# Two pairs with unscaled queries, a last pair normalized bank by bank, and conversions that begin one quarter sooner

## The chip, the cores and the metric

The kernel runs on one core of one Trainium2 chip. The metric is the time of the core on the device in microseconds, the median of three runs. Times of the trace are counted from the start of the profiled span.

## The reference, cut to what matters

Three stages follow each other: causal attention over 2 x 12 heads of 448 tokens, a soft mixture of 8 experts over the 896 tokens, and a gated feed-forward stage. What the change touches is the first one:

```python
scores = scale * np.matmul(q, k.transpose(0, 1, 3, 2))      # scale = 1/sqrt(64) = 0.125
scores = np.where(mask, -1000000000.0, scores)
scores = scores - np.max(scores, axis=-1, keepdims=True)
attn = np.exp(scores)
attn = attn / (np.sum(attn, axis=-1, keepdims=True) + 1e-09)
return np.matmul(attn, v)
```

The inputs are float32. The weights of the feed-forward stage (`wab`, `wo`) reach the kernel as 64-bit words.

## The kernel before, in words

**Pairs and quarters.** Attention works on 12 pairs of heads, one head in partitions 0 to 63 and one in 64 to 127. A pair's score matrix has seven blocks of 64 query rows, i = 0 to 6, of 64(i+1) columns each, packed into four PSUM banks, `BANKS = ((6, 0), (5, 1), (4, 2), (3,))`. The loop over `it` (0 to 12) and `g` (0 to 3) is written out in a fixed order (manual schedule): what stands first in the program runs first on its engine. One turn (it, g), below a quarter, computes bank g of pair `it` and turns a quarter of pair it-1:

- `scores`: a bf16 matmul puts the mask into the bank, TensorE (PE) adds q times k, and VectorE (DVE) takes the negated maximum of each block into `nm` (line 261).
- `softmax`: ScalarE (ACT) writes exp(score + nm) into `p` and the row sums into `sm` (line 273).
- `norm`: DVE makes the reciprocals `rc` (lines 285, 286), GpSimd (POOL) multiplies the blocks of `p` by them (line 289). At g = 2 blocks of banks 0 and 1 are normalized together, at g = 3 those of bank 2, and bank 3 in the next pair's quarter 0.
- `transp`: PE transposes four 128x128 blocks of the pair before into a PSUM tile `t`, in the order `TORD = (1, 3, 0, 2)`. `t_1` needs blocks 4, 5, 6, 2 of `p`; `t_3` blocks 4, 5, 6; `t_0` and `t_2` also need block 3, which is bank 3. ACT evicts three of the four to `pT` (line 307), DVE evicts `t_3` at the end of quarter 1 (line 311).
- `pv`, `xtr`, `logits`: PE multiplies `pT` with v two pairs behind (in four steps kt; the second reads `t_2`, the last two read `t_3`), transposes the result and adds to the logits of the experts.

**Queries.** `begin(it)` multiplies q by 0.125 in place (line 236): DVE does it for pair 0, POOL for the others, one pair ahead.

**Conversions.** The 64-bit weight words are widened to fp32 in between. One conversion of a raw tile is two ACT passes of 128x768 (lines 163, 164) and, one conversion later (`LAG = 1`), two DVE passes (lines 194, 197). `conv_step` is called in every quarter after the first `CVOFF`, and three of four quarters hold one conversion (`CVN`): the first of 32 in quarter (1, 3), the last in (12, 0). A conversion behind (11, 3) uses POOL instead of ACT (lines 156, 159). A raw tile that DVE is done with frees a slot, and `pump` issues the next load on the SP queue, in a fixed order: raw tiles 0 to 31, then the experts' weights `w`.

**The start.** SP issues q and k of pair 0, v, a raw tile, a `w`, q and k of pair 1, and more. PE first runs 32 `warm` matmuls on a bf16 copy of the identity (`ident16`, made by DVE on line 105), then the scores of pair 0, and four `warm` matmuls ahead of each quarter of pair 1.

**Behind attention.** `pv(11)`, `xtr(11)`, the last logits and the softmax over tokens follow each other down to `ssum` (line 587), the experts' input, and then the experts run on `w` tiles as they arrive. Two of the slots for `w`, t0 and t1, open where the tiles that `ssum` reads are closed, so that the SP queue, which is in order, waits for `ssum` there.

Of the kernel before, what the change touches and what calls it, by code (L numbers as in the profile page):

```python
# [15 lines left out]
ALU = mybir.AluOpType  # L16
# [3 lines left out]
S = 448  # L20
# [3 lines left out]
BANKS = ((6, 0), (5, 1), (4, 2), (3,))  # L24
# [13 lines left out]
TDVE = 1  # L38
# [4 lines left out]
    (("rect", 28, 4, 0, 28), ("tri", 6, 2), ("sq", 28, 4)),  # L43
    (("sq", 8, 16),),
)
CVOFF = 7
NWARM = 32
NW2 = 4
LAG = 1
# [40 lines left out]
def moe_kernel(ctx: ExitStack, tc: tile.TileContext, pk, vt, phi, w1, w2, wab, wo, rsel, out):  # L90
# [137 lines left out]
    def begin(it):  # L228
        d = st[it]
        d["nm"] = ap.tile([128, 8], F32, tag="nm", bufs=2, name=f"nm{it}")  # L230
        d["sm"] = ap.tile([128, 8], F32, tag="sm", bufs=2, name=f"sm{it}")
        d["rc"] = ap.tile([128, 8], F32, tag="rc", bufs=2, name=f"rc{it}")
        d["p"] = p_bufs[it % 2]
        q = d["qk"][:, 0:S]
        eng = nc.gpsimd if it else nc.vector
        eng.tensor_scalar(out=q, in0=q, scalar1=0.125, scalar2=1.0, op0=ALU.mult, op1=ALU.mult)

    def scores(it, g):
        d = st[it]
        qT, kT = d["qk"][:, 0:S], d["qk"][:, S:2 * S]  # L240
        tl = BANKS[g]
        sb = psS.tile([128, 512], F32, tag="s", name=f"s{it}_{g}")
        offs = [0, 64 * (tl[0] + 1)]
        w = 448 - 64 * tl[0]
        if len(tl) == 2:
            dg = sb[:, 512 - 2 * w:512].rearrange("p (j c) -> p j c", j=2)[:, :, w - 64:w]
            mk = mask16.unsqueeze(1).to_broadcast([128, 2, 64])
        else:
            dg, mk = sb[:, 64 * tl[0]:64 * tl[0] + 64], mask16
        nc.tensor.matmul(dg, lhsT=ident16, rhs=mk, start=True, stop=False, skip_group_check=True)  # L250
        for i, o in zip(tl, offs):
            n = 64 * (i + 1)
            for h in range(2):
                r = slice(64 * h, 64 * h + 64)
                nc.tensor.matmul(  # L255
                    sb[r, o:o + n], lhsT=qT[r, 64 * i:64 * i + 64], rhs=kT[r, 0:n],
                    start=False, stop=True, skip_group_check=True,
                )
        for i, o in zip(tl, offs):
            c = CIX[i]  # L260
            nc.vector.tensor_reduce(  # L261
                out=d["nm"][:, c:c + 1], in_=sb[:, o:o + 64 * (i + 1)], axis=AX.X, op=ALU.max, negate=True
            )
        d["s", g] = sb

    def softmax(it, g):
        d = st[it]
        tl = BANKS[g]
        sb = d.pop(("s", g))
        for i, o in zip(tl, (0, 64 * (tl[0] + 1))):  # L270
            n = 64 * (i + 1)
            c = CIX[i]
            nc.scalar.activation(  # L273
                out=d["p"][:, POFF[i]:POFF[i] + n], in_=sb[:, o:o + n], func=AF.Exp,
                bias=d["nm"][:, c:c + 1], scale=1.0, accum_out=d["sm"][:, c:c + 1],
            )

    def norm(it, tl):
# [15 lines left out]
    def transp(it, b):  # L294
        d = st[it]
        if b == TORD[0]:
            d["pT"] = ap.tile([128, 16, 128], F32, tag="pT", bufs=1, name=f"pT{it}")
        ps = psT.tile([128, 4, 128], F32, tag="t", name=f"t{it}_{b}")
        for j in range(4):
            kt, i = TBLK[4 * b + j]  # L300
            o = POFF[i] + 128 * kt
            nc.tensor.transpose(ps[:, j, :], d["p"][:, o:o + 128], ident)  # L302
        dst = d["pT"][:, 4 * b:4 * b + 4, :]
        if b == TORD[TDVE]:
            d["pt"] = dst, ps
        else:
            nc.scalar.activation(out=dst, in_=ps, func=AF.Copy)  # L307
# [190 lines left out]
    with tc.manual_schedule():  # L498
# [15 lines left out]
        for it in range(13):  # L514
            if 1 <= it < 12:
                load_v(it)
            for g in range(4):
                if it == 1:
                    warmup(NW2)
                if it < 12:  # L520
                    scores(it, g)
                if g == 0 and it >= 2:
                    pv(it - 2)
                if it >= 1:
                    transp(it - 1, TORD[g])
                if it < 12:
                    softmax(it, g)
                if g:
                    if it < 12:
                        norm(it, ((), BANKS[0] + BANKS[1], BANKS[2])[g - 1])  # L530
                elif it:
                    norm(it - 1, BANKS[3])
                if g == SCQ and it + 1 < 12:
                    begin(it + 1)
                if g == 3 and it + 2 < 12:
                    load_qk(it + 2)
                if (it, g) in DSP:
                    dispatch0(DSP.index((it, g)))
                if it >= 2 and g == (3 if it == 8 else 1):
                    xtr(it - 2)  # L540
                if it in (4, 7, 10) and g == 2:
                    logits((it - 4) // 6, (0, 1, 2) if it != 7 else (3, 4, 5))
                step += 1
                if step > CVOFF:
                    conv_step(CVN[step % len(CVN)], LAG, NT1, "pool" if (it, g) > LASTQ else "act")
                if g == TDVE and it >= 1:
                    evict(it - 1)
        pv(11)
        xtr(11)
# [742 lines left out]
```

## Time and profile before

| | |
|---|---|
| median of 3 runs | 373.66 us (372.74 to 375.65) |
| the profiled execution's own time | 373.79 us |
| its span, first to last instruction | 371.9 us |
| PE busy | 331.1 us (89%) |
| DVE busy | 228.9 us (62%) |
| ACT busy | 201.3 us (54%) |
| POOL busy | 94.1 us (25%) |
| DMA | 242 GB/s from and to HBM over the span |
| chain that ended last, by engine | PE 40%, ACT 21%, DVE 20%, DMA 12% |

The span and the profiled execution's time differ by 1.9 us that lie outside the instructions. A share of busy time is a mean over stages: in attention ACT and DVE are at work nearly all the time (24 to 130 us), in the experts' stage DMA is (140 to 270 us). A row of the timeline begins with start and duration in us; in brackets stands the idle time before it and what ended it.

### The profile page before, as it was taken

The numbers are of one execution on the slowest core, as the hardware profiler recorded it, in microseconds if no ns is written. First come the engines' busy times: TensorE is split into PE (matmuls) and PEld (weight loads), VectorE is DVE, ScalarE is ACT, GpSimd is POOL, SyncE is SP. The second block draws the span as 40 slices with busy tenths as digits, with TensorE's granted clock in tenths as the row PEclk, the third lists the DMA queues.
The fourth block names the chain that finished last, engine by engine and source line by source line (L and its number), as shares of the span: only waits on it lengthen the run. The fifth ranks groups of instructions, "written<-read, shape, count | busy, mean of one in ns | idle before, by whom it ended". The sixth has DMA issues, their size and how long they took to land.

```text
span 371.9 us, 6880 instructions
## 1 busy us (share of the span) xinstructions
PE 331.1 (89%) x2551; PEld 199.9 (54%) x2551; DVE 228.9 (62%) x610; ACT 201.3 (54%) x463; POOL 94.1 (25%) x131
## 2 busy tenths in 40 slices
PE   5898898989989978988978879999899889999995
PEld 4454444544544544433332337634565359889995
DVE  2579999999999972021015897507956669933121
ACT  1589999999999952103007445414546732423221
POOL 2446675666767550001000000000000110301110
PEclk9999999999999999999999999999999899999999
DMA  7738799999777779999999999787910000001222
GB/s 279 269 96 305 278 341 363 345 344 316 248 282 275 239 252 398 364 418 418 415 341 378 380 377 364 248 331 274 422 70 2 0 1 2 0 2 42 85 86 85
DMA packets 20224, 90.51 MB, mean 243 GB/s; under 512 B 2336, under 2 KB 5024, under 8 KB 20192
## 3 DMA queue, kind: packets, MB, share of 16 engines
q1 hardware_dynamic: 20192, 90.09, 65.1%
q8 instruction: 20, 0.33, 0.3%
q14 instruction: 12, 0.10, 0.1%
HBM read 87.33 MB, written 2.75 MB: 242 GB/s over the span
## 4 chain that ended last, share of the span: by engine, by line
PE 40%; ACT 21%; DVE 20%; DMA 12%; issue 3%; POOL 3%; ACTq 0%; DVEq 0%; SPq 0%; POOLq 0%
DMA w<-in_w_dram 12%; PE o L1165 8%; PE M L884 7%; ACT p L273 6%; DVE pf L826 4%; PE ab L770 4%; PE s L255 3%; ACT raw L164 3%; ACT wab L163 3%; PE h L644 3%; DVE pt L825 3%; PE so L685 3%; ACT pT L307 2%; POOL p L289 2%; DVE pf L837 2%
## 5 line engine op out<-in xcount | busy, mean ns | idle before, releaser
L289 POOL TENSOR_SCALAR p<-p,rc 128x448 f32<-128x448 f32 (+6 forms) x84 | 70.1, 848 | 33.2 <-DVE rc L286 26.9
L1069 POOL TENSOR_TENSOR cc<-gt,cc 128x512 fp32r<-128x512 f32 (+1 forms) x6 | 7.0, 1174 | 158.0 <-ACT cc L1068 158.0
L255 PE MATMUL s<-qk 64*64 64x448 f32 (+6 forms) x336 | 47.0, 392 | 0.0
L273 ACT ACTIVATE p<-s,nm 128x448 f32<-128x448 f32 (+6 forms) x84 | 40.3, 499 | 9.3 <-DVE nm L261 9.1
L884 PE MATMUL M<-wt,P_t 128*128 128x384 f32 x168 | 35.3, 351 | 4.4 <-DVE wt L879 1.4
L302 PE MATMUL t<-ident,p 128*128 128x128 f32 x192 | 33.3, 289 | 4.8 <-POOL p L289 4.1
L261 DVE TENSOR_REDUCE nm<-s 128x1 f32<-128x448 f32 (+6 forms) x84 | 31.7, 411 | 8.9 <-PE s L255 8.9
L194 DVE SCALAR_TENSOR_TENSOR raw<-raw 128x768 int32<-128x768 int32 x36 | 34.7, 963 | 3.7 <-ACT raw L164 1.8
L884 PEld LDWEIGHTS M<-wt,P_t 128*128 128x128 f32 x168 | 28.4, 188 | 13.0 <-ACT wt L878 3.9
L338 PE MATMUL v<-pT,v 128*64 128x448 f32 (+3 forms) x192 | 27.2, 396 | 9.0 <-ACT pT L307 7.2
L164 ACT ACTIVATE raw<-raw 128x768 int32<-128x768 uint32 x35 | 33.2, 949 | 0.0
L644 PE MATMUL h<-w,sT 128*32 128x512 f32 x192 | 29.1, 600 | 4.3 <-DMA w<-in_w_dram 3.3
L255 PEld LDWEIGHTS s<-qk 64*64 64x64 f32 x336 | 19.5, 133 | 19.9 <-issue 14.4
L302 PEld LDWEIGHTS t<-ident,p 128*128 128x128 f32 x192 | 20.4, 140 | 17.5 <-POOL p L289 6.4
L879 DVE TENSOR_TENSOR wt<-wo,wt 128x384 fp32r<-128x384 f32 x48 | 23.8, 551 | 7.9 <-ACT wt L878 7.9
L197 DVE SCALAR_TENSOR_TENSOR wab<-wab,raw 128x768 int32<-128x768 int32 x24 | 28.1, 1172 | 0.8
L878 ACT ACTIVATE wt<-wo 128x384 fp32r<-128x384 f32 x48 | 21.8, 513 | 12.5 <-PE M L884 12.2
L770 PE MATMUL ab<-wab,sT 128*32 128x384 f32 x288 | 27.2, 491 | 0.5 <-DVE sT L609 0.5
L685 PE MATMUL so<-w,hpad 128*32 128x384 f32 x256 | 24.6, 493 | 1.5 <-DMA w<-in_w_dram 0.7
L307 ACT ACTIVATE pT<-t 128x512 f32<-128x512 f32 x36 | 22.5, 625 | 4.1 <-PE t L302 3.8
L338 PEld LDWEIGHTS v<-pT,v 128*64 128x64 f32 (+1 forms) x192 | 10.8, 134 | 23.9 <-ACT pT L307 13.2
L163 ACT ACTIVATE wab<-raw 128x768 f32<-128x768 f32 x24 | 23.4, 975 | 0.0
(156 smaller groups left out, 520.2 us busy)
## 6 DMA issues: line engine op xcount, KB each, us to landing
w<-in_w_dram SPq DMA_DIRECT2D x64, 768.0 KB, 8.3
raw<-in_wab_dram SPq DMA_DIRECT2D x24, 768.0 KB, 5.3
raw<-in_wo_dram SPq DMA_DIRECT2D x12, 768.0 KB, 4.4
qk<-in_pk_dram SPq DMA_DIRECT2D x12, 448.0 KB, 5.0
v<-in_pk_dram SPq DMA_DIRECT2D x12, 192.0 KB, 4.5
out_dram<-ost SPq DMA_DIRECT2D x6, 384.0 KB, 2.3
v<-in_vt_dram SPq DMA_DIRECT2D x12, 32.0 KB, 4.3
out_dram<-ost SPq DMA_DIRECT2D x2, 192.0 KB, 1.9
```

The costliest lines, as they stand in the source:

```text
L163: nc.scalar.activation(out=dst, in_=hi, func=AF.Copy, scale=2.0 ** -112)
L164: nc.scalar.activation(out=pr[:, :, 0], in_=lw, func=AF.Copy, scale=2.0 ** -29, bias=-0.49999)
L194: nc.vector.scalar_tensor_tensor(out=b, in0=ph, scalar=-0x80000000, in1=b, op0=ALU.bitwise_and, op1=ALU.bitwise_or)
L255: nc.tensor.matmul(sb[r, o:o + n], lhsT=qT[r, 64 * i:64 * i + 64], rhs=kT[r, 0:n], start=False, stop=True, skip_group_check=True,)
L273: nc.scalar.activation(out=d["p"][:, POFF[i]:POFF[i] + n], in_=sb[:, o:o + n], func=AF.Exp, bias=d["nm"][:, c:c + 1], scale=1.0, accum_out ...
L289: nc.gpsimd.tensor_scalar(out=p[:, POFF[i]:POFF[i] + n], in0=p[:, POFF[i]:POFF[i] + n], scalar1=rc[:, CIX[i]:CIX[i] + 1], scalar2=1.0, op0 ...
L302: nc.tensor.transpose(ps[:, j, :], d["p"][:, o:o + 128], ident)
L338: nc.tensor.matmul(ps[r, 128 * kt:S], lhsT=lhsT, rhs=rhs, start=(kt == 0), stop=(kt == 3), skip_group_check=True)
L644: nc.tensor.matmul(ps[32 * g:32 * g + 32, :], lhsT=sT[:, 0, c, :], rhs=wt[8 * e + i // 3][:, 512 * (i % 3):512 * (i % 3) + 512], start=(i ...
L685: nc.tensor.matmul(so[32 * g:32 * g + 32, 0:384], lhsT=t[:, c, :], rhs=wt[8 * e + 4 + i // 4][:, 384 * (i % 4):384 * (i % 4) + 384], start ...
L770: nc.tensor.matmul(abps[q][32 * g:32 * g + 32, 0:384], lhsT=sT[:, 1, c, :], rhs=w[:, c % 2, 384 * g:384 * g + 384], start=(c == 0), stop=( ...
L884: nc.tensor.matmul(mps[k][h][:, 0:384], lhsT=l[:, f, :], rhs=r, start=(n == 0 and i == 0), stop=(n == 11 and i == 2))
```

## The change

For pairs 0 and 1 (`NRAW = 2`) the queries stay unscaled; each bank's `nm` is multiplied by 0.125 on DVE (a 128x1 or 128x2 instruction), and the exp gets the scale 0.125. The last pair is normalized bank by bank, bank 0 in quarter 1, bank 1 in quarter 2, bank 2 in quarter 3, bank 3 as before. The last pair's `t_3` and `t_2` are evicted by DVE right behind their transposes, the other two by ACT. `CVOFF` is 6 in place of 7, so that each conversion comes one converting quarter sooner.

```diff
--- before.py
+++ after.py
@@ -43,7 +43,8 @@
     (("rect", 28, 4, 0, 28), ("tri", 6, 2), ("sq", 28, 4)),
     (("sq", 8, 16),),
 )
-CVOFF = 7
+CVOFF = 6
+NRAW = 2
 NWARM = 32
 NW2 = 4
 LAG = 1
@@ -231,9 +232,10 @@
         d["sm"] = ap.tile([128, 8], F32, tag="sm", bufs=2, name=f"sm{it}")
         d["rc"] = ap.tile([128, 8], F32, tag="rc", bufs=2, name=f"rc{it}")
         d["p"] = p_bufs[it % 2]
-        q = d["qk"][:, 0:S]
-        eng = nc.gpsimd if it else nc.vector
-        eng.tensor_scalar(out=q, in0=q, scalar1=0.125, scalar2=1.0, op0=ALU.mult, op1=ALU.mult)
+        d["scale"] = 0.125 if it < NRAW else 1.0
+        if it >= NRAW:
+            q = d["qk"][:, 0:S]
+            nc.gpsimd.tensor_scalar(out=q, in0=q, scalar1=0.125, scalar2=1.0, op0=ALU.mult, op1=ALU.mult)
 
     def scores(it, g):
         d = st[it]
@@ -261,6 +263,9 @@
             nc.vector.tensor_reduce(
                 out=d["nm"][:, c:c + 1], in_=sb[:, o:o + 64 * (i + 1)], axis=AX.X, op=ALU.max, negate=True
             )
+        if it < NRAW:
+            c = d["nm"][:, CIX[tl[0]]:CIX[tl[0]] + len(tl)]
+            nc.vector.tensor_scalar(out=c, in0=c, scalar1=0.125, scalar2=None, op0=ALU.mult)
         d["s", g] = sb
 
     def softmax(it, g):
@@ -272,7 +277,7 @@
             c = CIX[i]
             nc.scalar.activation(
                 out=d["p"][:, POFF[i]:POFF[i] + n], in_=sb[:, o:o + n], func=AF.Exp,
-                bias=d["nm"][:, c:c + 1], scale=1.0, accum_out=d["sm"][:, c:c + 1],
+                bias=d["nm"][:, c:c + 1], scale=d["scale"], accum_out=d["sm"][:, c:c + 1],
             )
 
     def norm(it, tl):
@@ -301,7 +306,9 @@
             o = POFF[i] + 128 * kt
             nc.tensor.transpose(ps[:, j, :], d["p"][:, o:o + 128], ident)
         dst = d["pT"][:, 4 * b:4 * b + 4, :]
-        if b == TORD[TDVE]:
+        if it == 11 and b in (TORD[1], TORD[3]):
+            nc.vector.tensor_copy(out=dst, in_=ps)
+        elif it < 11 and b == TORD[TDVE]:
             d["pt"] = dst, ps
         else:
             nc.scalar.activation(out=dst, in_=ps, func=AF.Copy)
@@ -527,7 +534,7 @@
                     softmax(it, g)
                 if g:
                     if it < 12:
-                        norm(it, ((), BANKS[0] + BANKS[1], BANKS[2])[g - 1])
+                        norm(it, BANKS[g - 1] if it == 11 else ((), BANKS[0] + BANKS[1], BANKS[2])[g - 1])
                 elif it:
                     norm(it - 1, BANKS[3])
                 if g == SCQ and it + 1 < 12:
@@ -543,7 +550,7 @@
                 step += 1
                 if step > CVOFF:
                     conv_step(CVN[step % len(CVN)], LAG, NT1, "pool" if (it, g) > LASTQ else "act")
-                if g == TDVE and it >= 1:
+                if g == TDVE and 1 <= it < 12:
                     evict(it - 1)
         pv(11)
         xtr(11)
```

DVE at the start of the program (`nm0` and `s0_g` are pair 0's maxima and score banks). Before:

```order
L236 TENSOR_SCALAR qk0_143<-qk0_143 128x448
L105 CAST ident16_78<-ident_73 128x128
L115 COPY selsum_89<-ident_73 128x32
L128 TENSOR_TENSOR sel_88<-ident_73 128x32 x2
L117 TENSOR_TENSOR selsum_89<-selsum_89,ident_73 128x32 x3
L121 COPY selsum_89<-selsum_89 128x32 x3
L124 TENSOR_TENSOR sel16_97<-selsum_89 128x16 x6
L261 TENSOR_REDUCE nm0_193<-s0_0_197 128x1 x2
L261 TENSOR_REDUCE nm0_193<-s0_1_207 128x1 x2
```

Now:

```order
L106 CAST ident16_78<-ident_73 128x128
L116 COPY selsum_89<-ident_73 128x32
L129 TENSOR_TENSOR sel_88<-ident_73 128x32 x2
L118 TENSOR_TENSOR selsum_89<-selsum_89,ident_73 128x32 x3
L122 COPY selsum_89<-selsum_89 128x32 x3
L125 TENSOR_TENSOR sel16_97<-selsum_89 128x16 x6
L263 TENSOR_REDUCE nm0_193<-s0_0_196 128x1 x2
L268 TENSOR_SCALAR nm0_193<-nm0_193 128x2
L263 TENSOR_REDUCE nm0_193<-s0_1_207 128x1 x2
L268 TENSOR_SCALAR nm0_193<-nm0_193 128x2
```

The multiplication of the queries is gone from the head of DVE's program, so that the cast of the identity is its first instruction; a small multiplication stands behind each bank's maxima.

ACT in the quarters (1, 2) and (1, 3) (`raw0` and `raw1` are raw tiles, `s1_g` pair 1's score banks, `t0_b` pair 0's transposes). Before:

```order
L273 ACTIVATE p1_134,sm1_218<-s1_2_304,nm1_217 128x320
L273 ACTIVATE p1_134,sm1_218<-s1_2_304,nm1_217 128x192
L307 ACTIVATE pT0_264<-t0_2_335 128x512
L273 ACTIVATE p1_134,sm1_218<-s1_3_330,nm1_217 128x256
L163 ACTIVATE wab0_108<-raw0_182 128x768
L164 ACTIVATE raw0_182<-raw0_182 128x768
L342 ACTIVATE xT0_370<-v0_361 128x448
```

Now:

```order
L278 ACTIVATE p1_134,sm1_219<-s1_2_308,nm1_218 128x320
L278 ACTIVATE p1_134,sm1_219<-s1_2_308,nm1_218 128x192
L164 ACTIVATE wab0_108<-raw0_182 128x768
L165 ACTIVATE raw0_182<-raw0_182 128x768
L314 ACTIVATE pT0_267<-t0_2_343 128x512
L278 ACTIVATE p1_134,sm1_219<-s1_3_337,nm1_218 128x256
L164 ACTIVATE wab0_108<-raw1_188 128x768
L165 ACTIVATE raw1_188<-raw1_188 128x768
L349 ACTIVATE xT0_384<-v0_375 128x448
```

One conversion more stands ahead of the first copy of `pv` (`xT0`).

DVE at the end of attention, from pair 11's third pair of reciprocals on (`rc11`; `raw29` to `raw31` are the last raw tiles, `pT11` the last pair's evictions). Before:

```order
L285 TENSOR_SCALAR rc11_1392<-sm11_1391 128x2
L286 RECIPROCAL rc11_1392<-rc11_1392 128x2
L194 SCALAR_TENSOR_TENSOR raw29_1432<-raw29_1432 128x768
L197 SCALAR_TENSOR_TENSOR wo2_1490<-wo2_1490,raw29_1432 128x768
L285 TENSOR_SCALAR rc11_1392<-sm11_1391 128x1
L286 RECIPROCAL rc11_1392<-rc11_1392 128x1
L194 SCALAR_TENSOR_TENSOR raw30_1454<-raw30_1454 128x768
L197 SCALAR_TENSOR_TENSOR wo3_1563<-wo3_1563,raw30_1454 128x768
L194 SCALAR_TENSOR_TENSOR raw31_1495<-raw31_1495 128x768
L197 SCALAR_TENSOR_TENSOR wo3_1563<-wo3_1563,raw31_1495 128x768
L311 COPY pT11_1618<-t11_3_1638 128x512
```

Now:

```order
L290 TENSOR_SCALAR rc11_1405<-sm11_1404 128x2
L291 RECIPROCAL rc11_1405<-rc11_1405 128x2
L195 SCALAR_TENSOR_TENSOR raw30_1444<-raw30_1444 128x768
L198 SCALAR_TENSOR_TENSOR wo3_1555<-wo3_1555,raw30_1444 128x768
L195 SCALAR_TENSOR_TENSOR raw31_1467<-raw31_1467 128x768
L198 SCALAR_TENSOR_TENSOR wo3_1555<-wo3_1555,raw31_1467 128x768
L290 TENSOR_SCALAR rc11_1405<-sm11_1404 128x1
L291 RECIPROCAL rc11_1405<-rc11_1405 128x1
L310 COPY pT11_1636<-t11_3_1646 128x512
L310 COPY pT11_1636<-t11_2_1664 128x512
```

The passes of raw 31 stand ahead of bank 3's reciprocal now, not behind it; raw 31's ACT passes are in quarter (11, 3), and POOL has no conversion any more.

## Rows read from the trace of the kernel before

**Rows 1.** Windows: us, busy us of each engine, granted clock, DMA share, GB/s.

```profile
12.00:24.00 12.00, 10.38 (x89) 5.94 (x89) 6.61 (x25) 8.49 (x29) 6.75 (x15) 1.00 0.46 156
24.00:110.00 86.00, 77.25 (x587) 40.81 (x584) 82.64 (x160) 84.78 (x204) 55.48 (x64) 1.00 0.85 303
```

**Rows 2.** Timeline of the start: start us, us, engine, line, what, count, idle before.

```profile
1.14 0.29 POOL masks.py:199 TENSOR_SCALAR_AFFINE_SELECT ident<-ident 128x128 f32<-128x128 f32 x1
...
3.87 0.39 DVE L236 TENSOR_SCALAR qk<-qk 128x448 f32<-128x448 f32 x1 [3.87 <-DMA qk<-in_pk_dram]
4.18 0.22 DVE L105 CAST ident<-ident 128x128 bf16<-128x128 f32 x1
...
4.45 3.60 PE L504 MATMUL warm<-ident 128*128 128x128 bf16 x32 [4.45 <-DVE ident L105]
...
8.09 1.39 PE L255 MATMUL s<-qk 64*64 64x448 f32 x8
...
9.56 1.08 PE L255 MATMUL s<-qk 64*64 64x384 f32 x8
...
11.35 0.56 POOL L236 TENSOR_SCALAR qk<-qk 128x448 f32<-128x448 f32 x1 [8.71 <-DMA qk<-in_pk_dram]
...
13.15 3.20 POOL L289 TENSOR_SCALAR p<-p,rc 128x448 f32<-128x448 f32 x7 [1.23 <-DVE rc L286]
...
15.55 0.73 PE L302 MATMUL t<-ident,p 128*128 128x128 f32 x4 [1.62 <-POOL p L289]
```

**Rows 3.** Groups by line and shape, DVE's small instructions: busy us, mean ns.

```profile
L285 DVE TENSOR_SCALAR rc<-sm 128x2 f32<-128x2 f32 x12 | 5.2, 431 | 0.8 <-ACT p L273 0.8
...
L285 DVE TENSOR_SCALAR rc<-sm 128x1 f32<-128x1 f32 x12 | 1.7, 139 | 0.0
```

**Rows 4.** Timeline of ACT, quarters (1, 2) to (2, 1).

```profile
20.56 0.52 ACT L273 ACTIVATE p<-s,nm 128x320 f32<-128x320 f32 x1
...
22.43 0.93 ACT L163 ACTIVATE wab<-raw 128x768 f32<-128x768 f32 x1
...
24.59 0.54 ACT L342 ACTIVATE xT<-v 128x448 f32<-128x448 f32 x1 [0.43 <-PE v L338]
...
26.62 0.91 ACT L163 ACTIVATE wab<-raw 128x768 f32<-128x768 f32 x1
...
28.19 0.59 ACT L273 ACTIVATE p<-s,nm 128x384 f32<-128x384 f32 x1
```

**Rows 5.** Timelines of DVE and of POOL in pair 2.

```profile
24.19 0.96 DVE L194 SCALAR_TENSOR_TENSOR raw<-raw 128x768 int32<-128x768 int32 x1 [0.61 <-ACT raw L164]
...
28.34 0.76 DVE L261 TENSOR_REDUCE nm<-s 128x1 f32<-128x320 f32 x2 [0.69 <-PE s L255]
...
23.75 0.48 POOL L289 TENSOR_SCALAR p<-p,rc 128x256 f32<-128x256 f32 x1 [0.30 <-DVE rc L286]
```

**Rows 6.** Timeline of attention's end.

```profile
132.76 1.12 DVE L197 SCALAR_TENSOR_TENSOR wo<-wo,raw 128x768 int32<-128x768 int32 x1
...
134.95 1.51 PE L338 MATMUL v<-pT,v 128*64 128x448 f32 x8
...
135.65 0.96 DVE L194 SCALAR_TENSOR_TENSOR raw<-raw 128x768 int32<-128x768 int32 x1 [1.76 <-POOL raw L159]
...
137.51 0.68 DVE L311 COPY pT<-t 128x512 f32<-128x512 f32 x1
...
138.25 0.81 PE L338 MATMUL v<-pT,v 128*64 128x192 f32 x8 [1.79 <-DVE pT L311]
```

**Rows 7.** Groups by line and shape, POOL's bank 3.

```profile
L289 POOL TENSOR_SCALAR p<-p,rc 128x256 f32<-128x256 f32 x12 | 11.7, 973 | 8.7 <-DVE rc L286 6.7 <-ACT xT L342 1.9
```

**Rows 8.** Waits of the SP queue: waited for, us, times, longest.

```profile
SPq L471 <- DVE ssum L587: 7.7, 1, 7.7
```

**Rows 9.** Windows, columns as in rows 1: experts' first loads, and a stretch at the lower clock.

```profile
148.00:150.00 2.00, 1.58 (x19) 1.20 (x20) 0.73 (x2) 0.00 (x0) 0.00 (x0) 1.00 0.87 261
...
295.50:300.00 4.50, 4.50 (x22) 1.42 (x21) 1.79 (x3) 2.16 (x5) 2.53 (x2) 0.63 0.00 0
```

## The prediction

> **What bounds the kernel now.** I read the windows by stage first, then the timelines at both ends of attention, since a change that leaves the middle as it is can pay only there. In the middle ACT is busy 84.78 of 86 us and DVE 82.64 [rows 1]: these two set the pace of pairs 2 to 11, and the work that they get in a quarter there is the same before and after. From 12 to 24 us ACT is busy 8.49 of 12 us and DVE 6.61 [rows 1]: there is room, and something else holds the chain. The reader is to see what [rows 2]: the identity is ready at 1.43 us on POOL, but DVE's first instruction waits until 3.87 us for the queries' DMA, the cast of the identity stands behind it at 4.18, and PE's 32 warm matmuls begin at 4.45. So the scores begin at 8.09, although the queries had landed at 3.87. At the other end [rows 6], DVE waits 1.76 us for POOL's conversion of raw 31, its two passes run from 135.65 to 137.5, the eviction of `t_3` stands behind them, and PE waits 1.79 us for it; `pv(11)` ends at 138.25 + 0.81 = 139.06. What follows is one chain to `ssum`, and the SP queue waits 7.7 us for that [rows 8] before it issues the loads of the DMA-bound stage. What attention's end gains, the rest should gain as a block.
>
> **The change, step by step.** Times of the new kernel are worked out on the old clock.
>
> *Start.* With the queries' multiplication gone, the cast can begin when POOL has the identity, at about 1.45 (1.14 + 0.29), and PE at about 1.45 + 0.27 = 1.75 (4.45 less 4.18 is 0.27) [rows 2]. That is 2.7 us sooner. Warm-up lasts 3.6 us, the queries are there (3.87), so pair 0's scores begin at 8.09 - 2.7 = 5.4. Each bank's maxima are then followed by a small multiplication. No such instruction is in the trace; the nearest are the 128x1 and 128x2 additions of line 285, 0.14 and 0.43 us [rows 3]. The second includes stretches in which POOL works beside it, which it does not do here, so I take 0.17. In pair 0's pipeline PE needs 1.08 us a bank [rows 2] against about 0.9 on DVE, so only about one such instruction stands on the path (bounds 0.14 and 2 x 0.43). The reciprocals, and with them POOL's first normalization, move from 13.15 to 10.7. Seven blocks take 3.20 us; `t_1`, which waited 1.62 us for them, moves from 15.55 to 13.1: a gain of 2.45. Pair 1's queries still land at 11.35, as SP's first issues don't change; its scores can begin then without POOL's 0.56 us, and `t_1` at 13.1 stays the later one. From there PE's order sets the pace of pair 1, so that ACT's exp of (1, 2) begins at 20.56 - 2.45 = 18.1 [rows 4].
>
> *First conversion.* From 20.56 to 22.43 ACT does the exps of (1, 2), an eviction and the exp of (1, 3), 1.87 us; then one conversion, and the copy of `pv(0)` at 24.59, after 0.43 us of waiting for PE [rows 4]. A conversion takes 28.19 - 26.62 = 1.57 us from start to start [rows 4]. Now two of them stand ahead of that copy: 18.1 + 1.87 + 2 x 1.57 = 23.1 against 24.59. `pv(0)` needs `t_2`'s eviction, which is now behind the first conversion, and is done at about 22.6, so the copy does not wait. So 1.4 to 1.5 us of the 2.45 are left; I take 1.4. DVE has its own queue: raw 0's two passes move into (1, 3), ahead of the maxima of (2, 0); raw 1's can begin behind those (from 20.7, 0.96 + 1.12 us), the maxima (0.76) and a reciprocal (0.3), at about 23.9, where raw 0's began at 24.19 [rows 5, 6]: only 0.3 us sooner. But behind them DVE waited 0.69 us for PE at 28.34 and 0.61 us for ACT [rows 5], and takes these back. Bounds of this step: 0.3 (DVE keeps the pace) and 2.45 (conversion hidden). From here ACT and DVE have the same work in each quarter as before until raw 31's ACT passes end, in (11, 3), where raw 30's ended. The loads of raw tiles move by one tile in SP's order and are issued at the same events.
>
> *End.* Reciprocals bank by bank add two small instructions in (11, 1) (0.14 to 0.6 us, on DVE where ACT does not wait; I take nothing, 0.6 if that cover is gone). POOL begins pair 11's blocks earlier, and `t_1` and `t_3` no longer wait for them. Raw 31's passes on DVE now end where raw 30's did, at 132.76 + 1.12 = 133.9 [rows 6]. Behind them stand bank 3's reciprocal (0.3 us, to 134.2) and POOL's multiplication of that block. This is late: before, the reciprocal stood ahead of raw 30's passes; `t_0` and `t_2` now wait for it. It costs 0.48 us when no two-input DVE pass runs beside it [rows 5], 0.97 in the mean [rows 7]. DVE's long passes are over, so 0.48: 134.7. Then the last block of `t_0` and the four of `t_2` (0.73 us for four [rows 2]), 135.6; `t_2`'s eviction on DVE, 0.68 as `t_3`'s [rows 6], 136.3; and of `pv(11)` three of four steps, about half of 1.51 less its wait, 0.6, and 0.81: 137.7. PE's fillers and the first step stand in between; I take 137.9 to 138.0. Against 139.06 that is a gain of 1.1 (0.5 with a slow POOL).
>
> The rows' 0.48 and 0.97 have a rule beside them: the Trainium skill, "SBUF — State Buffer", section "Who interferes with whom", says that a VectorE instruction with two SBUF inputs holds off a GpSimd instruction that reads SBUF. By it the last block is multiplied undisturbed here, and the sum is the one with 0.48; without it, 0.5 us more. The trace agrees, as the 0.48 us stand where DVE's pass had not begun.
>
> *Rest.* The weights' loads w8 to w11 are issued about a quarter earlier, since raws 28 to 31 are done earlier. They are not waited for in the first experts, so nothing is gained from them alone; the DMA-bound stage begins when `ssum` opens the next slots [rows 8], and moves with it.
>
> *Sum.* 1.4 + 1.1 = 2.5 us. Against the profiled execution's own 373.79 us (373.66 in the median) that is **371.3 us**.
>
> **Rivals.**
> - *One end only.* DVE stays 0.3 us ahead and no more, or POOL is slow at the end: 0.3 + 1.1 or 1.4 + 0.5, so 371.9 to 372.4. For it: DVE is 96% busy in the middle [rows 1]. Against: 3.4 us of idle time there take up the 1.1 us.
> - *The conversion is hidden.* 2.45 + 1.1 = 3.55, so 370.2. ACT has 3.5 us of idle time in 12 to 24 us [rows 1], but most of it lies ahead of (1, 2).
> - *The start does nothing beyond attention.* If the experts' loads were bound by the DMA queue rather than by `ssum`, 373.7 to 373.8. Against: SP sits 7.7 us on that wait [rows 8], and at 148 to 150 us DMA's share falls to 0.87 with 261 GB/s [rows 9], less than in attention [rows 1], so the queue had run dry.
> - *Slower.* PE now has a gap of about 1.2 us between pair 0's scores (done at about 10) and the landing of pair 1's queries at 11.35, and one of 2 us before bank 3's block. The granted clock can fall: from 295.5 to 300 it is 0.63 [rows 9], part of the stretch at 1.2 GHz in place of 2.4 GHz. At the lower level PE's work takes twice as long, so each us of it costs up to 0.5 us; it decides when more than 5 us of PE's path run at that level. If pairs 0 and 1 ran so throughout, PE's 10.38 us in 12 to 24 us [rows 1] would become 20.8 and the time 371.3 + 10.4 = 381.7. A part of it gives 374 to 376. Against: PE waited 1.62 us at 15.55 and 1.79 us at 138.25 without such a loss [rows 2, 6]. The Trainium skill, "TensorE: Matmul & The Clock Gate", Part 1, says that the lower level is the default and that activity releases it; by it these gaps are what to look at. The first bank of scores taking 1.39 us and the second 1.08 [rows 2] agrees with a rise in between.
>
> **How the numbers follow.** Forecast 55% (370.7 to 371.8), one end only 20%, hidden conversion 10%, nothing beyond attention 9%, slower 6%. The range 369.9 to 373.2 leaves out the last two. One per cent, 3.7 us, is about what a measurement of this kernel can tell from no change; faster than that takes both upper bounds at once and a little more: 7%. Slower than that needs the long stretch at the lower clock: 3%. Within 1%: 90%.
>
> **What would show it.** PE's warm matmuls begin near 1.75 us and the first scores near 5.4; `t_1` of pair 0 near 13.1; ACT's first copy of `pv` near 23.1; DVE's last raw pass about 1.4 us before 133.9; `pv(11)` ends near 136.5; `ssum` and all that follows come about 2.5 us sooner, at unchanged lengths. I am wrong if the copy at 23.1 is near 24.5 (the start's gain is eaten), if DVE's passes in pairs 3 to 11 run at the old times, if PE waits for `t_0` past 134 us, or if the granted clock falls below 1 in the first 25 us.

## Result and the profile after

The changed kernel took 371.40 us in the median of 20 runs (368.80 to 374.41), against 374.87 for the kernel before beside it: 0.9916 of its time, 95% interval 0.9891 to 0.9941, so 2.2 to 4.1 us less. 371.3 us were predicted. That forecast and median lie 0.1 us apart is in part luck: the forecast took 2.5 us off the 373.7 to 373.8 us of the kernel before, which took 1.1 to 1.2 us more beside the changed one, and more than 2.5 us were gained. The profiled execution took 372.12 us (span 370.0), against 373.79 (371.9).

One thing is needed to read these numbers. Each run comes with the mean clock that TensorE was granted in it (a share of its upper level: 1 at 2.4 GHz, 0.5 at 1.2 GHz), and its time goes with that: over the 219 runs whose clock is on record (the 20 of the kernel before beside the changed one are not among them), a mean clock lower by 0.01 goes with 2.98 +- 0.13 us more (a straight line, each kernel with its own offset, 1.0 us left over). Below, "at the same clock" is that offset against the kernel before; its standard error is 0.3 us (0.4 for e9 and e10), and +- always means one such error. For the changed kernel the offset is -3.1 us. The ratios leave out the 21 runs that came over 1.5% above the fastest of their kernel, which the medians and the line hold; without them the line's slope is 2.54, e4's offset -2.6 in place of -2.2, and no other moves by more than 0.2 us.

The windows of the changed kernel (us, busy us of PE, PEld, DVE, ACT, POOL, granted clock, DMA share, GB/s), which answer to [rows 1, 9], with two around 45 us:

```profile
12.00:24.00 12.00, 10.19 (x89) 5.95 (x87) 7.75 (x23) 8.65 (x24) 5.80 (x13) 1.00 0.59 217
24.00:110.00 86.00, 77.22 (x574) 40.86 (x571) 82.69 (x164) 84.47 (x203) 57.10 (x64) 0.98 0.85 303
...
148.00:150.00 2.00, 1.89 (x21) 0.83 (x24) 0.36 (x1) 0.00 (x0) 0.00 (x0) 1.00 0.93 298
...
40.00:45.00 5.00, 3.53 (x28) 1.50 (x25) 4.90 (x8) 5.00 (x12) 4.54 (x6) 1.00 0.62 200
45.07:48.48 3.41, 3.41 (x16) 1.96 (x17) 3.09 (x8) 3.29 (x8) 2.05 (x2) 0.50 1.03 404
```

The middle is as it was, DVE and ACT full, but from 45.07 to 48.48 us the clock stood at its lower level (0.50; below, such a drop is called a fall). In the profile before it did not do so there.

The start of the changed kernel, in order of time (it answers to [rows 2]):

```profile
1.47 0.23 DVE L106 CAST ident<-ident 128x128 bf16<-128x128 f32 x1 [1.47 <-POOL ident masks.py:199]
...
1.75 3.60 PE L511 MATMUL warm<-ident 128*128 128x128 bf16 x32 [1.75 <-DVE ident L106]
...
5.39 1.97 PE L257 MATMUL s<-qk 64*64 64x448 f32 x8
...
7.51 1.08 PE L257 MATMUL s<-qk 64*64 64x384 f32 x8
...
11.31 2.74 POOL L294 TENSOR_SCALAR p<-p,rc 128x448 f32<-128x448 f32 x6 [8.60 <-DVE rc L291]
...
13.70 0.73 PE L307 MATMUL t<-ident,p 128*128 128x128 f32 x4 [1.51 <-POOL p L294]
```

PE begins 2.70 us sooner, and the first scores do too, but their first bank takes 1.97 us in place of 1.39, at the lower clock (the trace records no clock ahead of its rise, at 7.52 us here and 8.73 us before; the bank's length shows it). `t_1` has gained 1.85 us. What the first conversion leaves of it, on ACT and DVE [rows 4, 5]:

```profile
18.72 0.52 ACT L278 ACTIVATE p<-s,nm 128x320 f32<-128x320 f32 x1
...
23.79 0.52 ACT L349 ACTIVATE xT<-v 128x448 f32<-128x448 f32 x1
...
21.38 1.21 DVE L195 SCALAR_TENSOR_TENSOR raw<-raw 128x768 int32<-128x768 int32 x1 [1.18 <-ACT raw L165]
...
24.43 0.96 DVE L195 SCALAR_TENSOR_TENSOR raw<-raw 128x768 int32<-128x768 int32 x1
```

The exp of (1, 2) is 1.84 us sooner, the copy of `pv(0)` 0.80. DVE's first pass of raw 1 begins at 24.43 us, 0.24 us later than raw 0's did, but from 32 to 45 us DVE's maxima are 0.88 us sooner too, so DVE did not hold the kernel to its old pace. Attention's end, in order of time [rows 6]:

```profile
132.97 0.96 DVE L198 SCALAR_TENSOR_TENSOR wo<-wo,raw 128x768 int32<-128x768 int32 x1
133.84 0.14 DVE L290 TENSOR_SCALAR rc<-sm 128x1 f32<-128x1 f32 x1
...
134.35 0.48 POOL L294 TENSOR_SCALAR p<-p,rc 128x256 f32<-128x256 f32 x1 [3.54 <-DVE rc L291]
...
134.88 0.77 PE L307 MATMUL t<-ident,p 128*128 128x128 f32 x5 [1.45 <-POOL p L294]
...
135.90 2.10 PE L345 MATMUL v<-pT,v 128*64 128x448 f32 x16
```

SP's wait for `ssum` (total us, times, longest), which answers to [rows 8]:

```profile
SPq L478 <- DVE ssum L594: 9.6, 1, 9.6
```

`pv(11)` ends at 138.00, 1.06 us sooner, though raw 31's conversion on ACT ended where raw 30's did before (131.93 and 131.73).

How far instructions of the same place stand from the kernel before, followed through both traces: -1.84 at the exp of (1, 2); -0.80 at the copy of `pv(0)`; -0.88 up to 45 us; +0.37 behind the fall; 0.00 from 68 to 115 us; +0.25 at 131; -1.06 at `pv(11)`'s end and unchanged from there to 190 us; -1.75 at 193; -2.74 at 214; -1.64 behind another fall at 215.7; -1.67 at the end.

### The profile page after: what moved, and what is told of

Same layout as the page of the kernel before. It is cut to its first block, busy times and chain, and to the rows that moved or that the text cites. A ratio compares the mean times of both kernels' runs of the same rounds, so it can differ in the third digit from the quotient of the medians.

```text
span 370.0 us, 6891 instructions
## 1 busy us (share of the span) xinstructions
PE 334.6 (90%) x2551; PEld 201.8 (55%) x2551; DVE 230.1 (62%) x620; ACT 202.0 (55%) x464; POOL 91.1 (25%) x128
## 4 chain that ended last, share of the span: by engine, by line
PE 46%; ACT 27%; DVE 16%; issue 4%; DMA 3%; POOL 3%; ACTq 0%; POOLq 0%; DVEq 0%
ACT p L278 8%; PE o L1172 8%; PE M L891 8%; PE h L651 5%; PE so L692 4%; ACT raw L165 4%; PE ab L777 4%; ACT wab L164 4%; DVE pf L833 3%; ACT pT L314 3%; PE s L257 3%; DVE pt L832 3%; DMA raw<-in_wo_dram 3%; POOL p L294 3%; ACT wo L164 2%
## 5 line engine op out<-in xcount | busy, mean ns | idle before, releaser
L294 POOL TENSOR_SCALAR p<-p,rc 128x448 f32<-128x448 f32 (+6 forms) x84 | 69.2, 837 | 46.4 <-DVE rc L291 36.9
L257 PE MATMUL s<-qk 64*64 64x448 f32 (+6 forms) x336 | 48.5, 403 | 0.1
L651 PE MATMUL h<-w,sT 128*32 128x512 f32 x192 | 29.9, 614 | 3.2 <-DMA w<-in_w_dram 2.3
L314 ACT ACTIVATE pT<-t 128x512 f32<-128x512 f32 x35 | 21.7, 619 | 5.5 <-PE t L307 5.0
```

Of the source, the lines that this page charges most:

```text
L257: nc.tensor.matmul(sb[r, o:o + n], lhsT=qT[r, 64 * i:64 * i + 64], rhs=kT[r, 0:n], start=False, stop=True, skip_group_check=True,)
L294: nc.gpsimd.tensor_scalar(out=p[:, POFF[i]:POFF[i] + n], in0=p[:, POFF[i]:POFF[i] + n], scalar1=rc[:, CIX[i]:CIX[i] + 1], scalar2=1.0, op0 ...
L651: nc.tensor.matmul(ps[32 * g:32 * g + 32, :], lhsT=sT[:, 0, c, :], rhs=wt[8 * e + i // 3][:, 512 * (i % 3):512 * (i % 3) + 512], start=(i ...
```

## The experiments

All kernels stood beside the kernel before on the same chip. The ratio is to its runs there; the last column is the difference at the same clock, in us. Code is cut to what matters.

| kernel | median us | ratio (95%) | same clock |
|---|---|---|---|
| changed kernel | 371.40 | 0.9916 (0.9891 to 0.9941) | -3.1 |
| e1, queries only | 371.21 | 0.9930 (0.9892 to 0.9968) | -3.0 |
| e2, conversions only | 372.99 | 0.9985 (0.9949 to 1.0021) | -0.5 |
| e3, end only | 374.91 | 1.0022 (0.9987 to 1.0058) | +0.1 |
| e4, loads held | 372.90 | 0.9955 (0.9916 to 0.9994) | -2.2 |
| e6, without the new end | 370.22 | 0.9900 (0.9866 to 0.9933) | -3.4 |
| e8, queries, ACT evicts | 370.06 | 0.9903 (0.9873 to 0.9933) | -3.4 |
| e9, one unscaled pair | 374.16 | 0.9995 (0.9950 to 1.0041) | -1.4 |
| e5, reciprocal between | 370.25 | 0.9897 (0.9862 to 0.9932) | -4.0 |
| e11, fillers | 369.88 | 0.9883 (0.9849 to 0.9916) | -3.5 |
| e10, banks ahead | 366.69 | 0.9819 (0.9765 to 0.9874) | -5.4 |

### The three parts, each alone (e1, e2, e3) and the end left out (e6)

e1, against the kernel before:

```
+NRAW = 2          # and its uses; CVOFF = 7, attention's end as before
```

> The kernel before with the unscaled queries of pairs 0 and 1 alone; conversions begin where they did, attention's end is as before. Theory N (new: the start is worth what its t_1 gained, 1.85 us, less what the first conversion eats; the other half of the gain is made in the DMA-bound stage, because the loads w4 to w11 are issued 3 us sooner, by the earlier conversions): the first conversion stays one quarter later than in the changed kernel and eats nothing, so attention's chain keeps 1.85 us, and w4 to w11 move by the same, so the DMA-bound stage gives nothing more: 1.6 to 1.9 us less than before. Theory P (as predicted, the loads' place is worth nothing, the whole gain is made by both ends of attention): the same, up to 2.45 us less. Theory C (the difference of the two kernels is the number of stretches at the lower granted clock): no difference beyond 0.5 us.

e2 (queries scaled as before, by DVE for pair 0):

```
-CVOFF = 7
+CVOFF = 6
```

> The kernel before with the conversions begun one quarter sooner (CVOFF 6) alone; queries scaled as before, attention's end in the old order. At the start the first conversion costs 1.0 us of attention's chain; at its end DVE's wait of 1.76 us for POOL's conversion of raw 31 is gone, worth 1.4 to 1.7. Theory P: 0.4 to 0.7 us less than before. Theory N: w4 to w11 are issued some 2 to 3 us sooner, the queue is empty by ssum, and 1.7 us more are gained behind it: 2.0 to 2.5 us less than before, with DMA's share from 146 to 150 us near 0.5 in place of 0.94. Theory C: no difference beyond 0.5 us.

e3:

```
+norm(it, BANKS[g - 1] if it == 11 else ...)
+if it == 11 and b in (TORD[1], TORD[3]): nc.vector.tensor_copy(out=dst, in_=ps)
...
```

> The kernel before with the new end of attention alone (pair 11 normalized bank by bank, t_3 and t_2 evicted by DVE), conversions and queries as before. Raw 31's passes on DVE still end near 137.5 us, and both evictions now stand behind them: t_3 at 138.2, t_2 at 138.8, pv(11) 0.5 to 0.7 us later than before. Theories N and P: 0.3 to 0.8 us more than before, so this part is worth something only together with the earlier conversions. If the bank-wise normalization itself were worth the tail's gain: 0.5 to 1 us less.

e6 is the changed kernel without these lines:

> The changed kernel with attention's end as before (pair 11 normalized in the old groups, t_3 alone evicted by DVE, at the end of its quarter). The conversions alone moved pv(11)'s end from 2.4 us behind the kernel before to 1.05 behind, without the new end. Theory N: the new end is worth 0 to 0.3 us on top, so this kernel is within 0.4 us of the changed one, and 2.7 to 3.2 us below the kernel before at the same clock. Theory P (1.1 us of the gain need the new order at the end): 0.8 to 1.1 us above the changed kernel.

e1 alone gives what the whole change gives, -3.0 us, where 1.6 to 1.9 were expected and 2.45 at most. In its profile 1.86 us were gained at the first exp of pair 1, until the clock fell at 13.7 us, which cost 1.35 of it. e2 shows both sides of the early conversion: the copy of `pv(0)` comes 1.21 us later than before (0.16 us of it stood at the exps of pair 1 already), `pv(11)`'s end gains 1.35 on the copy of `pv(10)`. The end of e2, DVE in order of time:

```profile
134.08 0.96 DVE L195 SCALAR_TENSOR_TENSOR raw<-raw 128x768 int32<-128x768 int32 x1 [0.37 <-ACT raw L165]
135.08 0.96 DVE L198 SCALAR_TENSOR_TENSOR wo<-wo,raw 128x768 int32<-128x768 int32 x1
...
136.22 0.67 DVE L316 COPY pT<-t 128x512 f32<-128x512 f32 x1
```

DVE's wait of 1.76 us for POOL's conversion [rows 6] is 0.37 here, with the old evictions. The new ones alone (e3, DVE again) put both copies behind the late passes:

```profile
136.84 0.96 DVE L198 SCALAR_TENSOR_TENSOR wo<-wo,raw 128x768 int32<-128x768 int32 x1
137.72 1.28 DVE L310 COPY pT<-t 128x512 f32<-128x512 f32 x2
```

e3 came out even where 0.3 to 0.8 us more were expected; its interval does not exclude that. e6 lies 0.2 us from the changed kernel, within the error: the new end shows no worth on top of the conversions. The gain at attention's end is made by `CVOFF`, not by the order of evictions. e2 gave 0.5 us, as by theory P (0.4 to 0.7), though its interval holds 0 too. The 2.0 to 2.5 us that the place of the loads was to give did not come, although DMA's share from 146 to 150 us fell to 0.39, as that theory said: `ssum` itself came 1.05 us later than before there.

### Does the place of the loads count (e4, e8)?

e4, the changed kernel with

```
+def touch(i):
+    nc.vector.tensor_copy(out=touched[:, i - 28:i - 27], in_=raw[i][:, 0:1])
+    used("raw", i)
...
```

> The changed kernel with the loads of w4 to w11 held back: each ring slot of raws 28 to 31 is read once more by a copy of one column on DVE, behind the next raw tile's passes (raw 31's behind attention), so that w4 to w7 are issued about as late as in the kernel before and w8 to w11 behind them; the conversions and attention keep their places but for the four short copies (0.1 us each, three of them on the way). Theory P: the loads' place costs nothing, so it stays 2.8 to 3.3 us below the kernel before, as the changed kernel did (371.40 against 374.87). Theory N: the queue is not empty at ssum, DMA's share from 146 to 150 us is near 0.9 again and not 0.51, and 1.4 to 1.9 us of the gain are gone: 1.2 to 1.9 us below the kernel before.

e8, e1 with

```
-if b == TORD[TDVE]:
+if it < 11 and b == TORD[TDVE]:
...
```

> Unscaled queries of pairs 0 and 1, conversions and normalization as before, and only this at the end: all four blocks of pair 11 are evicted by ACT, so that t_3 no longer stands behind raw 31's passes on DVE. Without the wait of 1.79 us for that copy, pv(11) ends some 1.8 us sooner than with the queries alone, ssum as well. The loads w4 to w11 stay where the queries alone put them. Theory P (what ssum gains, the rest gains as a block): 1.6 to 1.9 us below the kernel with the queries alone, near 369.2 us at the same clock. Theory N (the loads ahead of ssum are a backlog in the queue; before, w11 landed at 151.0 and w12 at 153.6, while loads in a full queue land every 1.9 us, so only some 0.6 us of an earlier ssum are left to gain): 0.4 to 0.9 us below the kernel with the queries alone, and DMA's share stays near 1 through ssum.

The window from 146 to 150 us of the kernel before, the changed kernel and e4 (the last two numbers are DMA's share and GB/s):

```profile
146.00:150.00 4.00, 3.58 (x46) 2.24 (x42) 1.56 (x5) 0.00 (x0) 0.00 (x0) 1.00 0.94 337
146.00:150.00 4.00, 3.58 (x42) 2.24 (x42) 1.39 (x3) 0.00 (x0) 0.00 (x0) 1.00 0.51 162
146.00:150.00 4.00, 3.58 (x46) 2.25 (x42) 1.55 (x4) 0.00 (x0) 0.00 (x0) 1.00 0.93 334
```

The same window of e8:

```profile
146.00:150.00 4.00, 3.58 (x40) 1.95 (x41) 0.98 (x3) 0.00 (x0) 0.00 (x0) 1.00 1.01 414
```

The queue is full again in both. e4 lost 0.5 to 0.9 us (+- 0.4) against the changed kernel at the same clock, of which its short copies take up to 0.3, and the intervals of the two ratios overlap. At 2.2 to 2.6 us below the kernel before it lies between the two theories and decides neither. e8's trace shows how a backlog, loads issued and not yet landed, takes a gain. Its `ssum` came 1.72 us sooner than before, but SP then waited for landings, 10.0 us in all from 110 to 195 us, against 1.7 before (a row of SP's waits):

```profile
SPq L476 <- DMA w<-in_w_dram: 10.0, 10, 1.5
```

Landings of the experts' loads, taken from the trace's DMA issues (`w11` is the last that is issued ahead of `ssum`, `w12` the first behind it):

| | `ssum` against before | `w11` lands | `w12` lands | `w21` lands |
|---|---|---|---|---|
| before | | 151.0 | 153.6 | 170.9 |
| changed | -1.06 | 146.9 | 151.1 | 169.3 |
| e1 | -0.67 | 150.0 | 152.1 | 170.3 |
| e8 | -1.72 | 151.8 | 153.7 | 170.8 |
| e5 | -4.70 | 145.4 | 148.8 | 165.9 |

In a full queue loads of 768 KB land every 1.9 us. In e8 the loads ahead of `ssum` were still landing, so `w12` and all behind it came when before: the landings kept none of the 1.72 us, and of PE's lead, 1.72 us up to 184 us, 0.24 were left at 192. A fall at 11.55 us had put these loads 1.0 us later than before in this profile, so it shows more of a backlog than a run without that fall would. In the changed kernel the queue had run dry (DMA's share was 0.08 from 146 to 147 us), and `ssum`'s gain counted in full. e5 kept its 4.70 us up to 190 us too, but not everything against the changed kernel: its last load ahead of `ssum` landed 1.7 us behind `ssum`, and `w12` came only 2.3 us sooner than there, `ssum` 3.6. Over the runs e8 was 0.4 +- 0.4 us below e1 at the same clock, as the theory of the backlog said (0.4 to 0.9), not 1.6 to 1.9.

### The kernel before once more (b1)

> The kernel before, profiled a second time. In its first profile the last two of the DMA-bound stage's slower landings (the routing tensor at 197.5, 2.2 us behind the load ahead of it, and raw 35 at 205.8, 2.9 us behind) cost about 1.6 us that no other profile of these kernels shows. If they are a trait of this kernel, they are there again. If they are chance, the landings are 1.9 us apart there, the profiled time is 1.0 to 1.6 us lower at the same number of stretches at the lower clock, and what the first profile showed as a gain behind ssum is not the change's.

It took 374.09 us. The routing tensor landed 1.3 us behind the load ahead of it and raw 35 1.9 us: chance. At 212 us b1 stood 0.71 us ahead of the first profile (1.0 to 1.6 were expected), so that much of the -2.74 at 214 us above is not the change's. Then its clock fell at 217.2 us, where the first profile's did not; that cost 1.05 us.

### The second pair (e9)

```
-NRAW = 2
+NRAW = 1
```

> The changed kernel with unscaled queries for pair 0 alone (NRAW 1); POOL multiplies pair 1's queries again, when they land near 11.1 us, ahead of pair 0's first blocks in its queue. POOL's multiplication (0.56 us) and pair 1's scores behind it stand on the way to t_1, so t_1 of pair 0 moves from 13.7 to 14.2 to 14.3 and everything behind it by as much. If the second pair's queries were worth nothing, t_1 stays at 13.7. In time 0.5 us above the changed kernel by the first, none by the second.

POOL of e9 from 11 us:

```profile
11.44 0.56 POOL L238 TENSOR_SCALAR qk<-qk 128x448 f32<-128x448 f32 x1 [8.73 <-DMA qk<-in_pk_dram]
11.97 3.19 POOL L294 TENSOR_SCALAR p<-p,rc 128x448 f32<-128x448 f32 x7
```

It multiplies the queries first, and pair 0's blocks wait behind. `t_1` came at 14.37 us, near the 14.2 to 14.3 expected of a second pair that counts; the total came out as in the kernel before. At the same clock that is 1.7 us above the changed kernel, more than the 0.5 expected; the rest is not accounted for. The clock fell at 13.27 us in this profile, and the mean over its runs was 0.981, the lowest of all (before 0.987).

### PE's gaps and the clock (e11)

```
-if it == 1: warmup(NW2)
+if it == 1: warmup(NW2 + 6 if g == 0 else NW2)
+if (it, g) == (1, 0): warmup(12)      # ahead of t_1
```

> The changed kernel with 6 more warm matmuls ahead of pair 1's first bank and 12 more ahead of t_1 of pair 0 (0.1 us each at the upper clock), in PE's two gaps of the start. In 4 of 6 profiles with unscaled queries the granted clock fell to half between 11 and 15 us, in none of 4 with scaled ones, which have one gap there and not two. If the gaps let it fall: no fall between 9 and 18 us, the runs' mean granted clock 0.002 to 0.004 above the changed kernel's 0.986, and 0.3 to 1.0 us less in the median. If the falls come without regard to the gaps: the same mean clock within 0.001, and a time within 0.3 us of the changed kernel or up to 0.5 us more for the fillers.

The granted clock from 11 to 18 us was below 1 in 5 of 7 profiles with unscaled queries and no fillers (e1, e4, e6, e8, e9; not in the changed kernel and e5), in none of the 4 with scaled ones, and not in e11 or e10 (below). If falls had no regard to the kernel, 5 of 7 against 0 of 4 would come about once in 22 times. The worst is e8, where PE waited 2.69 us for pair 1's queries; its windows there:

```profile
11.00:13.00 2.00, 0.57 (x2) 0.29 (x4) 0.08 (x1) 0.10 (x2) 1.81 (x5) 0.64 1.04 426
13.00:15.00 2.00, 2.00 (x11) 1.14 (x8) 0.55 (x2) 0.00 (x0) 0.00 (x0) 0.50 0.98 391
15.00:17.00 2.00, 2.00 (x12) 1.17 (x12) 0.59 (x5) 1.51 (x5) 0.48 (x1) 0.50 0.50 186
```

It cost 3.9 us of its chain (-3.09 at 10.4 us, +0.84 at 19.3). e11's runs had a mean clock of 0.9895 (changed kernel 0.986, with a spread of 0.006 between runs) and a median 1.5 us lower: this speaks for the gaps, but the difference in clock is less than twice its error, and the kernel before and e1 do not differ in it (0.987 both). e11's profile decides nothing: the changed kernel's, with the same rise (7.5 and 7.6 us) and no fillers, has no fall there either. e6 has the same start and its rise at 7.47 us, and fell at 14.30. That the gaps let the clock fall is not shown.

### Two versions that go on from the changed kernel (e5, e10)

e5, the changed kernel with

```
 i, di, b, ph = fin.pop(0)
+if i == NT1 - 1: norm(11, BANKS[3])
-if it == 11 and b in (TORD[1], TORD[3]): nc.vector.tensor_copy(out=dst, in_=ps)
...
```

> The changed kernel with bank 3's reciprocal of pair 11 moved ahead of raw 31's two passes on DVE (behind raw 30's), and all four evictions of pair 11 on ACT, which is idle from 133.7 us there. The late step of the changed kernel is that reciprocal, at 133.84 behind raw 31's passes. It can be done at 131.7 to 132.0; POOL's last block then runs beside raw 31's passes and takes 1.0 to 1.5 us in place of 0.48, to 133.3; t_2 is evicted near 134.9 in place of 136.4, and pv(11) ends near 136.4 in place of 138.0. Theory N (a shift of ssum counts in full as long as the queue is empty by then, which it is, since w11 has landed at 146.9): 1.3 to 1.6 us below the changed kernel, 4.3 to 4.8 below the kernel before. Theory P2 (POOL is held off by DVE's two-input passes until they end near 134.3): at most 0.3 us below the changed kernel.

The end of e5 on DVE, then POOL:

```profile
129.43 0.14 DVE L292 TENSOR_SCALAR rc<-sm 128x1 f32<-128x1 f32 x1
...
129.87 0.96 DVE L197 SCALAR_TENSOR_TENSOR raw<-raw 128x768 int32<-128x768 int32 x1
130.86 1.13 DVE L200 SCALAR_TENSOR_TENSOR wo<-wo,raw 128x768 int32<-128x768 int32 x1
...
129.93 1.24 POOL L296 TENSOR_SCALAR p<-p,rc 128x256 f32<-128x256 f32 x1 [1.23 <-ACT raw L165]
```

`pv(11)`'s end gained 2.8 us on the copy of `pv(10)` (-1.90 at 131.6, -4.71 behind it), where the changed kernel gained 1.3. POOL's last block took 1.24 us beside DVE's passes in place of 0.48. The Trainium skill, "SBUF — State Buffer", section "Who interferes with whom", says that a VectorE instruction with two SBUF inputs contends with a GpSimd instruction that reads SBUF. The trace agrees that it costs, 0.76 us, and shows that the block ended before DVE's second pass did, against theory P2. At the same clock e5 is 0.9 +- 0.4 us below the changed kernel, less than the 1.3 to 1.6 of theory N; the backlog behind its `ssum`, seen above, may have kept the rest. The ratios of the two overlap.

e10, e5 with

```
+load_qk(1)        # right behind load_qk(0), ahead of pump(2)
-scores(it, g)     # for it == 1: one bank ahead
+if it == 1 and g < 3: scores(1, g + 1)
...
```

> The kernel with bank 3's reciprocal between the last raw passes, and two edits at the start: pair 1's queries are loaded right behind pair 0's, ahead of the first raw tiles, and pair 1's scores are issued one bank ahead, so that PE computes bank 1 while it waits for POOL's first blocks. If PE's order sets pair 1's pace: t_1 stays where POOL's blocks are ready (12.7 to 13.7), and t_3, t_0 and t_2 follow it 0.7 to 1.0 us sooner each than there; the exp of (1, 2) is sooner by 0.5 to 1.0 us, and the total by as much. PE's gaps ahead of t_1 shrink from 1.15 and 0.5 to 2.7 us to at most 1 us, so the granted clock should not fall between 9 and 18 us. If pair 0's queries land late because they share the DMA engines with pair 1's: the first scores come up to 1.5 us later, and the time is 0 to 1 us above.

The start of e10 on PE, pair 1's first two banks and `t_1`:

```profile
9.62 1.08 PE L259 MATMUL s<-qk 64*64 64x448 f32 x8
...
10.79 1.08 PE L259 MATMUL s<-qk 64*64 64x384 f32 x8
12.42 0.73 PE L309 MATMUL t<-ident,p 128*128 128x128 f32 x4 [0.54 <-POOL p L296]
```

PE's gaps ahead of `t_1` are down to 0.54 us, the exp of (1, 2) comes 3.6 us sooner than before, and 2.7 us are left behind the first conversion (1.8 in e5). The exp of (1, 2) is 0.75 us sooner than in e5, as expected, and there is no fall between 9 and 18 us. e10 took 366.69 us, 0.982 of the kernel before, in 6 runs; the ratio's interval ends at 0.987, below the changed kernel's, and its mean clock, 0.993, was the highest. At the same clock it is 1.4 +- 0.5 us below e5, where 0.5 to 1.0 were expected; its two edits were not run apart.

## Why the prediction was right, point by point

**What binds the start: right.** Cast at 1.47, warm matmuls at 1.75, first scores at 5.39 us, all as predicted.

**Its gain: mis-sized.** 2.45 us were predicted at `t_1`, 1.85 came. The step that failed is "times of the new kernel are worked out on the old clock". The clock rose at 8.73 us before and at 7.52 after, 1.2 us sooner although PE began 2.7 us sooner, and the first bank stood in the slow stretch: 1.97 us, 0.58 more than before. In e5 the rise came at 5.2 us, ahead of that bank, and `t_1` at 12.71, a gain of 2.84 (two rows of PE in e5):

```profile
5.33 1.08 PE L259 MATMUL s<-qk 64*64 64x448 f32 x8
...
12.71 0.73 PE L309 MATMUL t<-ident,p 128*128 128x128 f32 x4 [0.50 <-POOL p L296]
```

The Trainium skill, "TensorE: Matmul & The Clock Gate", Part 1, says that the monitor does not start anew with a kernel, so that the rise varies from run to run by 0.5 us either way. The profiles agree that it varies, but by more: it came from 4.6 to 7.6 us with unscaled queries, while PE began at 1.75 us in each.

**The first conversion: right.** It eats 1.0 us (1.84 to 0.80 after; 2.85 to 1.83 in e5; e2 lost 1.0 to 1.1).

**The pace of pairs 2 to 11: right up to the fall.** The gain stood at 0.88 us until the clock fell at 45 us, which took 1.25. The forecast had nothing for this. 0.37 came back at 61 us by chance of order: DVE's addition of 128x4 took 0.17 us in place of 0.53, since POOL's multiplication of the queries (60.87 to 61.43 us before) no longer lay beside it. Before and after:

```profile
60.93 0.53 DVE L285 TENSOR_SCALAR rc<-sm 128x4 f32<-128x4 f32 x1
61.30 0.17 DVE L290 TENSOR_SCALAR rc<-sm 128x4 f32<-128x4 f32 x1
```

**The end: right in size.** An end of `pv(11)` at 137.9 to 138.0 was predicted ahead of the start's gain. It came at 138.00 with attention 0.25 us late by then, so at 137.75 without that: a gain of 1.3 in place of 1.1 (POOL's block 0.48, as chosen). As far as the runs tell, all of it belongs to the earlier conversions (e2, e6), none to the bank-wise normalization and DVE's evictions. That 138.00 us is also the predicted number is luck: with 1.4 us of the start's gain the sum meant 136.5.

**The signs.** Two signs of being wrong came true in the profile: DVE's passes from 68 to 115 us ran at the old times, and PE waited for `t_0` until 134.88 us. Both follow from the fall at 45 us, which took the whole lead, and not from the steps of the sum; without its 1.25 us PE's wait would have ended near 133.6.

**The rest as a block: right up to the queue.** -1.06 from `pv(11)` to 190 us. What the prediction said of the loads, "nothing is gained from them alone", hid a condition: `ssum`'s gain counts only if the queue is all but empty when it comes. Its reading that the queue had run dry in the kernel before is wrong: `w11` landed there at 151.0 us, 2.6 us behind `ssum`, and DMA's share from 146 to 150 us was 0.94. The change empties the queue, since raws 28 to 31 are done 3 us sooner; e8, which does not, lost most of its gain there in its profile.

**The sum.** At the same clock the change is worth 3.1 us, 0.6 more than predicted. Followed in the profiles it is 0.85 + 1.3 at attention's ends, and 0.5 to 0.7 us of an empty queue (`w21` came 1.6 us and the work at 193 us 1.75 us sooner, `ssum` 1.06), a term that the prediction put at nothing. b1 agrees: it has the other two falls as well, and the changed kernel ended 1.97 us ahead of it with the 1.25 us of its fall at 45 us in that, so 3.2 us. e1 reaches the same 3.0 over its runs with about 1.9 us at the start and nothing of the rest; 1.2 us of it are not followed. The kernel before itself varies: at a mean clock of 0.995 its 14 runs lie between 371.06 and 374.48 us, and e1's two at 368.88 and 369.00, so 2.2 us below the lowest of them. What makes the others slower no trace shows, so how much of the 3.0 is the start's stays open, and with it how the whole divides between the three parts.

**The rival "slower by the clock": half right.** Falls do come near the gaps that it named, in 5 of 7 profiles, and cost 1.3 us (e1) to 3.9 us (e8) there. But the kernel before has its own, later, and the means of the runs hardly differ.

## What to carry to other kernels

A gain on an engine's chain counts up to the first place where another resource has a backlog: look at what the DMA queue still has to land when the waiting issue is released. Of a change of several parts, run each part alone: here one part gave as much as the whole, one gave back at its end what it took at its start, and one showed no worth. A forecast that meets the total may have met it by terms that are off on both sides. When one core's runs spread by 1%, compare them at the same granted clock before any term below that is believed.

## What the runs showed of the hardware

- The granted clock falls in the middle of a busy kernel: before the falls at 45.07, 215.7 and 294.2 us of the changed kernel PE had been busy 71% (40 to 45 us), 67% (210 to 215.5) and 78% (289 to 294) at the upper level. The kernel before was at 75% from 40 to 45 us and did not fall there. What decides is not settled here.
- What a fall costs depends on the stage: 1.25 us at 45 us, in attention; 1.36 us at 170.8 us in e1, of which all but 0.2 us was made good by 212 us (against b1), where the loads bind.
- A DVE addition of four columns took 0.17 us alone and 0.53 us beside POOL's multiplication of the queries.
- The clock's rise came from 4.6 to 7.6 us in nine profiles in which PE began at 1.75 us.
